# First MLP pair: weight decodes let go one block earlier, token sums spaced evenly from the first one on

## The chip, the cores and the metric

One Trainium2 chip, of which the kernel uses 1 core. The metric is device time in microseconds (us), the median of several executions. Engines are named as the profile names them: PE is TensorE (matmuls), PEld its weight loads, DVE is VectorE, ACT is ScalarE, POOL is GpSimd, SP is SyncE, which here only issues DMAs.

## The reference, cut to what matters

```python
x = attention(q, k, v, omega)            # linear attention, 2304 tokens x 512
xn = x / rms(x) * rms_g
x = (silu(xn @ w_gate) * (xn @ w_val)) @ w_out      # gated MLP, d_ff 1536
h = x @ w_in                                        # second MLP, d_ff 2048
return (h * sigmoid(h)) @ w_out
```

The weights come as 64-bit floats. The kernel reads them as pairs of 32-bit words and turns each 128 x 512 block into a float32 on the chip; this is the "decode" below.

## The kernel before, in words

The 2304 tokens are 18 tiles of 128, in five blocks: j = 0 to 3 with 512 tokens and j = 4 with 256. After attention the normalised tokens lie in `xs[j]` as a high and a low half, so that every product is three matmuls (high x high, high x low, low x high). The rest of the program is a list of groups: nine gated groups of one d_ff block each, then eight groups of the second MLP of two d_ff blocks each. The first two of the eight (`std`, `std + 1`, here called the first and the second MLP pair) are computed plainly. The others, and the gated ones before them, use `quad`: the products of blocks 0 and 1 (and of 2 and 3) are formed from sums and differences of tokens and of weights, with fewer matmuls. The sums of the finished tokens must therefore be made during the two plain pairs, by `token_sums`.

Three streams of side work are interleaved with the matmuls while the program is written out; each engine then runs its own instructions strictly in that written order.

- **Decodes.** `WeightQueue` holds a list of jobs. For one weight block, `dec` issues five DVE operations of 128 x 512 on `raw` and `m` (lines 146, 149, 152, 154, 157) and two POOL additions (L160); then `load` issues the DMA of a later block into the freed `raw` buffer on SP (L134 or L136). `hi` is a copy on ACT (L443) into a weight slot `w0_n` or `w1_n`, `lo` a subtraction on DVE (L447). Matmuls on that weight wait for `lo`. `wq.hold = True` stops jobs from being taken; `need` takes them regardless.
- **Token sums.** `token_sums` gives a list of steps on 128 x 1024: `whole` (DVE, L373), `minus` (DVE, L376), `tok_high` (ACT, L365) and `tok_low` (DVE, L368). They work in temporary slots: ('t', 0), ('t', 1) from the free weight slots, and `w1_7`.
- **The hidden layer.** For each product of 512 tokens, ACT takes the silu (L239 or L713) and a rounded copy (L198) and DVE the remainder (L199); the output matmuls (PE, L300) need both halves. Their results are copied by ACT (L317) to a staging buffer `ya`, which SP stores to HBM (L323) in the first pair and POOL adds to HBM afterwards (L325).

In the first pair the order on PE is: four plain blocks (`mlp_block`, j = 0 and 1), `g1_mlp` of block 2 for both d_ff blocks with the output of blocks 0 and 1 behind them, blocks 3 and 4, then the next pair. The main loop of the program walks `stream()`, whose values `c` are the estimated PE time of the next piece, and decides after each piece whether a sum and a job are taken:

```python
            due += c
            gone += c
            if sums and gone > wq.rest:
                sums.pop(0)()
                gone = gone - wq.rest if wq.rest not in (T_PACE, M_PACE + T_PACE) else 0.0
            if wq.hold:
                due = min(due, M_PACE)
            elif due > wq.pace and wq.tick():
                due = min(due - wq.pace, wq.pace)
```

Of the kernel before, what the change touches and what calls it, by code (L numbers as in the profile page):

```python
# [8 lines left out]
F32 = mybir.dt.float32  # L9
# [11 lines left out]
def kernel(  # L21
# [77 lines left out]
    def ps_tile(which, shape):  # L99
        p, tag, n = pools[which]  # L100
        return p.tile(shape, F32, tag=tag, name=tag, bufs=n)
# [91 lines left out]
    M_PACE, A_PACE, S_PACE, R_PACE, S_REST, T_PACE = 2.0, 1.8, 2.3, 2.0, 2.1, 1.2  # L193
# [39 lines left out]
    def g1_mlp(f, j, hs, mid, late):  # L233
        wq.need((2, "i", f))
        p = ps_tile("ps_g" if blocks[j] == TB * P else "ps_y", [P, blocks[j]])
        yield from proj(wt[2, "i", f], j, p)
        yield from late
        s = pools["s"][0].tile([P, blocks[j]], F32, tag="s", name="s", bufs=pools["s"][1])
        nc.scalar.activation(out=s, in_=p, func=AF.Silu)  # L239
        hs[f] = split_h(s, j)  # L240
        yield from mid
# [87 lines left out]
    tok, sums, ready, wait, stages = {}, [], set(), [], []  # L329
# [6 lines left out]
    std = next(u for u, g in enumerate(groups) if g[0] == 2)  # L336

    def w_tile(side, slot, dtype=F32R):
        pool = pools["w"][2] if side and slot < W_EARLY else pools["w"][side]
        return pool.tile([P, 2 * KC * P], dtype, tag=f"w{side}_{slot}", name=f"w{side}_{slot}")  # L340
# [233 lines left out]
    wq = WeightQueue()  # L574
# [151 lines left out]
    def stream():  # L726
        f0, (f2,) = sweeps[0][1], sweeps[1][1]
        pend = ()
        order = [(3, f0), (4, f0), (1, [f2]), (0, [f2]), (2, [f2]), (3, [f2]), (4, [f2])]
        def temp(k):  # L730
            if k == 2:
                return w_tile(1, 7, F32)
            return rawp.tile([P, KH * TB * P], F32, tag=f"raw{1 - k % 2}", name=f"raw{1 - k % 2}", bufs=1)

        def end(n):
            wq.load(0, n, n)
            wq.hold = n == 0
            wq.rest = T_PACE if wq.hold else M_PACE + T_PACE

        now, later = token_sums(0, temp, end, nc.gpsimd)  # L740
        sums.extend(now)
        for n, (j, fs) in enumerate(order):
            hs, mine = {}, n == len(order) - 1
            for f in fs:
                yield from g1_glu(f, j, hs, () if mine else pend)
                pend = pend if mine else ()
            if n == 2:
                sums.extend(later)
                wq.free += [(0, k) for k in range(6)]
            out = g2_glu(fs, j, hs, j >= NE and fs is f0, False)  # L750
            pend = chain_of(pend, out) if mine else out
        spent = [(1, k) for k in range(3)]
        for u, (kind, fs) in enumerate(groups):
            first, last = kind == 2 and fs[0] == 0, u == len(groups) - 1
            done = u + 1 == std
            wq.rest = S_REST
            wq.std = u < std + NSTD
            wq.pace = A_PACE if u < std else S_PACE if u < std + NSTD else R_PACE
            hs = {j: {} for j in range(NB)}
            if std <= u < std + NSTD:  # L760
                out_of = lambda j: g2_mlp(fs, j, hs[j], first, False, False)
                ys = iter(pend)
                wq.hold = first
                if first:
                    stages[:] = [ya[3][:, n * 1024:][:, :1024] for n in range(2)] + [ya[4]]
                while wait:
                    wait.pop(0)()
                each = [(2, 1), (2, 2), (1, 0), (2, 1)] if first else [(2, 2), (1, 1), (0, 0), (0, 0)]
                for n, k in enumerate(each):
                    if n == 2 and not first:  # L770
                        sums.extend(later + rest)
                    if n == 3:
                        if not first:
                            ys = chain_of(ys, out_of(1))
                        wq.release(*wq.keys(u - 1)[1])
                    j = n // 2 if first else 1 - n // 2
                    yield from mlp_block(fs[n % 2], j, hs[j], ys, k if n < 3 else (k[0], 9))
                yield from g1_mlp(fs[0], 2, hs[2], (), out_of(0) if first else ())
                wq.hold = False
                if first:  # L780
                    assert wq.jobs.pop(0)[0] == 1 << 10
                    now, later = token_sums(
                        0, lambda k: w_tile(1, 7, F32) if k == 2 else wq.slot(("t", k), F32), lambda n: None
                    )
                    sums.extend(now)
                    now, last1 = token_sums(
                        1,
                        lambda k: w_tile(*wq.held["t", 1 - k // 3], F32) if k in (0, 3)
                        else ya[2][:, :2 * KH * TB * P].rearrange("p (k n) -> p k n", k=2)[:, 2 - k],
                        lambda n: None if n else wq.release(("t", 0)),  # L790
                    )
                    sums.extend(now[:9])
                    rest = now[9:]
                yield from g1_mlp(fs[1], 2, hs[2], (), out_of(int(first)))
                yield from g1_mlp(fs[0], 3, hs[3], (), ())
                yield from g1_mlp(fs[1], 3, hs[3], (), out_of(2))
                if not first:
                    sums.extend(last1)
                for f in fs:
                    yield from g1_mlp(f, 4, hs[4], (), ())  # L800
                wq.release(*wq.keys(u)[0])
                pend = chain_of(out_of(3), out_of(4))
                continue
            yield from quad(u, iter(pend), hs)
            if u:
                wq.release(*wq.keys(u - 1)[1])
            else:
                wq.free += spent
            if kind == 1:
                f = fs[0]  # L810
                out_of = lambda j: g2_glu(fs, j, hs[j], False, done)
                ys = chain_of(out_of(0), out_of(1))
                yield from glu_block(f, 2, hs[2], ys, {"g": 0, "v": 1})
                yield from glu_block(f, 3, hs[3], ys, {"g": 1, "v": 1})
                yield from glu_block(f, 4, hs[4], ys, {"g": 1, "v": 1})
                yield from ys
                pend = chain_of(out_of(2), out_of(3), out_of(4))
                wq.release(*wq.keys(u)[0])
            else:
                out_of = lambda j, end=None: g2_mlp(fs, j, hs[j], False, last, end)  # L820
                if u == std + NSTD:
                    wq.release(("t", 1))
                yield from quad(u, chain_of(out_of(1), out_of(0)), hs, 1)
                if last:
                    *stages[:], o0, o1, o2 = [w_tile(1, k, F32) for k in range(3, 9)]
                    ends = [o.rearrange("p (t d) -> p t d", t=2) for o in (o0, o1, o2)]
                    for o, j, n in zip(ends, (4, 2, 2), (0, 0, 1)):
                        for p0, p1, rows in out_pair(j, n):
                            nc.sync.dma_start(out=o[p0:p1], in_=rows)
                    yield from g1_mlp(fs[0], 4, hs[4], (), out_of(3))  # L830
                    yield from g1_mlp(fs[1], 4, hs[4], (), ())
                    yield from chain_of(out_of(4, ends[:1]), out_of(2, ends[1:]))
                else:
                    yield from g1_mlp(fs[0], 4, hs[4], (), out_of(3))
                    yield from g1_mlp(fs[1], 4, hs[4], (), ())
                    wq.release(*wq.keys(u)[0])
                    pend = chain_of(out_of(2), out_of(4))
# [697 lines left out]
    with tc.manual_schedule():  # L1535
# [33 lines left out]
        first = idle(5, [])  # L1569
# [16 lines left out]
        n = 0  # L1586
        for j in range(NE):
            n = add_block(j, sweeps[0][1], n)
# [14 lines left out]
        due = gone = 0.0  # L1603
        for c in stream():
            due += c
            gone += c
            if sums and gone > wq.rest:
                sums.pop(0)()
                gone = gone - wq.rest if wq.rest not in (T_PACE, M_PACE + T_PACE) else 0.0
# [4 lines that stand above are left out]
# [30 lines left out]
```

## Time and profile before

| what | value |
|---|---|
| runs | 952.29 us median of 3 (950.94 to 954.12) |
| the profiled execution | 952.68 us, of which the span from first to last instruction is 950.9 us |
| PE busy | 936.9 us, 99% of the span |
| DVE busy | 699.7 us, 74% |
| ACT, POOL busy | 482.6 us (51%), 452.4 us (48%) |
| chain that ended last | PE 94%, DVE 3%, ACT 1%, issue 1% |
| mean granted clock of PE | 0.996 of full speed |

The page shows one execution. A busy PE there is a PE with matmuls in flight; where it is not busy, the views of waits and of windows tell what it stood waiting for.

### The profile page before, as it was taken

How to read it: one execution, taken by the hardware profiler on the slowest of the kernel's cores; microseconds unless marked ns; L12 is line 12 of the kernel's file. 1: busy time of each engine (PE TensorE's matmuls, PEld its weight loads, DVE VectorE, ACT ScalarE, POOL GpSimd, SP SyncE). 2: the span in 40 equal slices, each digit the busy share in tenths (PEclk: the TensorE clock that was granted, in tenths of full speed). 3: DMA queues.
4: the chain of work that ended last, by engine and by line, in shares of the span. 5: the costliest groups of instructions: out<-in, count | busy, mean ns of one | idle time of the engine just before them, and what ended most of it. 6: DMA issues, size and time to landing. Idle time of an engine off the chain costs nothing.

```text
span 950.9 us, 17234 instructions
## 1 busy us (share of the span) xinstructions
PE 936.9 (99%) x6534; PEld 785.9 (83%) x6534; DVE 699.7 (74%) x1330; ACT 482.6 (51%) x1066; POOL 452.4 (48%) x464
## 2 busy tenths in 40 slices
PE   8999999999999999999999999799999999999998
PEld 6888878888888888888888888688888888888887
DVE  6998989658687878779778787985575757575634
ACT  6999877543424323433333355466444544545442
POOL 8888655315445445426335202536454545454411
PEclk9999999999999999999999999899999999999999
DMA  8655443002111121021112102348768786878777
GB/s 197 166 135 142 137 125 101 12 23 78 56 45 45 45 67 45 23 66 49 41 45 65 47 1 77 123 118 170 142 127 170 128 168 130 162 142 153 116 146 168
DMA packets 89282, 95.03 MB, mean 100 GB/s; under 512 B 28400, under 2 KB 74736, under 8 KB 89200
## 3 DMA queue, kind: packets, MB, share of 16 engines
q1 hardware_dynamic: 79424, 62.41, 22.9%
q0 software_dynamic: 9504, 31.46, 19.8%
q8 instruction: 51, 0.84, 0.4%
q14 instruction: 31, 0.25, 0.1%
q10 hardware_dynamic: 272, 0.07, 0.0%
HBM read 51.45 MB, written 37.75 MB: 94 GB/s over the span
## 4 chain that ended last, share of the span: by engine, by line
PE 94%; DVE 3%; ACT 1%; issue 1%; DMA 0%; SPq 0%; DVEq 0%; ACTq 0%
PE g L580 21%; PE y L300 20%; PE g L205 18%; PE y L259 14%; PE y L205 6%; PE b L1112 4%; PE b L205 4%; PE kv L1192 2%; PE b L1512 2%; PE b L1296 2%; PE b L1085 2%; PE b L1392 1%; PE b L1272 1%; DVE w L373 0%; PE b L1553 0%
## 5 line engine op out<-in xcount | busy, mean ns | idle before, releaser
L160 POOL TENSOR_TENSOR m<-m,raw 128x512 int32<-128x512 int32 x136 | 195.2, 1435 | 210.0 <-issue 83.3
L300 PE MATMUL y<-w,h 128*128 128x512 f32 (+1 forms) x870 | 213.7, 390 | 2.1 <-DVE h L199 1.9
L300 PEld LDWEIGHTS y<-w,h 128*128 128x128 f32 x870 | 163.2, 189 | 36.7 <-DVE h L199 2.5
L205 PE MATMUL g<-xs,w 128*128 128x512 f32 x768 | 188.1, 391 | 4.1 <-DVE w L447 4.1
L205 PEld LDWEIGHTS g<-xs,w 128*128 128x128 f32 x768 | 143.8, 189 | 33.8 <-DVE w L447 4.5
L259 PE MATMUL y<-h,w 128*128 128x512 f32 (+1 forms) x648 | 155.5, 366 | 0.0
L199 DVE TENSOR_TENSOR h<-s,h 128x512 fp32r<-128x512 f32 (+1 forms) x134 | 104.9, 794 | 67.8 <-ACT h L198 66.6
L270 DVE TENSOR_TENSOR ya<-y,ya 128x512 f32<-128x512 f32 (+1 forms) x200 | 122.8, 631 | 20.9 <-PE y L259 20.5
L259 PEld LDWEIGHTS y<-h,w 128*128 128x128 f32 x648 | 113.2, 188 | 20.4 <-DVE h L199 0.5
L580 PE MATMUL g<-xs,w 128*128 128x512 f32 x504 | 128.2, 390 | 0.0
L198 ACT ACTIVATE h<-s 128x512 fp32r<-128x512 f32 (+1 forms) x134 | 77.1, 585 | 89.8 <-DVE s L692 49.4
L325 POOL DMA_DIRECT2D out_dram<-ya x64 | 59.3, 989 | 126.4 <-DVE ya L319 51.1
L580 PEld LDWEIGHTS g<-xs,w 128*128 128x128 f32 x504 | 94.1, 188 | 19.5
L317 ACT ACTIVATE ya<-y 128x512 f32<-128x512 f32 x82 | 48.8, 596 | 77.2 <-PE y L300 77.1
L319 DVE COPY ya<-y 128x512 f32<-128x512 f32 x52 | 35.8, 689 | 62.9 <-PE y L300 62.9
L1161 ACT ACTIVATE e<-b,nb 128x128 f32<-128x128 f32 x272 | 76.1, 425 | 7.6 <-issue 4.1
L447 DVE TENSOR_TENSOR w<-m,w 128x512 fp32r<-128x512 f32 x65 | 64.3, 991 | 13.3 <-ACT w L443 12.1
L580 PE MATMUL g<-w,w 128*128 128x512 f32 x270 | 68.8, 390 | 0.0
L605 ACT ACTIVATE s<-s 128x512 f32<-128x512 f32 x33 | 20.9, 632 | 88.9 <-DVE s L610 88.9
L205 PEld LDWEIGHTS y<-xs,w 128*128 128x128 f32 x480 | 61.5, 188 | 2.7
L205 PE MATMUL y<-xs,w 128*128 128x256 f32 x480 | 62.2, 280 | 0.0
L580 PEld LDWEIGHTS g<-w,w 128*128 128x128 f32 x270 | 50.1, 188 | 10.0
(136 smaller groups left out, 1340.1 us busy)
## 6 DMA issues: line engine op xcount, KB each, us to landing
out_dram<-ya POOLq DMA_DIRECT2D x52, 512.0 KB, 6.9
raw<-in_moe_w_out_dram SPq DMA_DIRECT2D x28, 512.0 KB, 4.1
raw<-in_moe_w_in_dram SPq DMA_DIRECT2D x16, 512.0 KB, 4.4
raw<-in_moe_w_gate_dram SPq DMA_DIRECT2D x12, 512.0 KB, 3.5
raw<-in_moe_w_val_dram SPq DMA_DIRECT2D x12, 512.0 KB, 3.6
qT<-e SPq DMA_DIRECT2D x72, 64.0 KB, 2.4
x<-in_k_dram SPq DMA_DIRECT2D x16, 256.0 KB, 3.8
x<-in_q_dram SPq DMA_DIRECT2D x16, 256.0 KB, 3.3
```

Of the source, the lines that this page charges most:

```text
L160: tt(out=mi, in0=mi, in1=(low if step == 5 else high).bitcast(I32), op=ALU.add)
L198: nc.scalar.activation(out=ht[:, 0, :], in_=s, func=AF.Copy)
L199: nc.vector.tensor_tensor(out=ht[:, 1, :], in0=s, in1=ht[:, 0, :].bitcast(F32), op=ALU.subtract)
L205: nc.tensor.matmul(out=ps, lhsT=w[:, a, cc * P:(cc + 1) * P], rhs=xs[j][:, c, cc, :], start=(n == 0), stop=(n == 3 * KC - 1),)
L259: nc.tensor.matmul(out=ps, lhsT=wt[1, "o", f][:, a, d * P:(d + 1) * P], rhs=hs[f][:, c, :], start=(n == 0), stop=(n == nn - 1),)
L270: nc.vector.tensor_tensor(out=y[:, d, :], in0=ps, in1=y[:, d, :], op=ALU.add)
L300: nc.tensor.matmul(out=ps, lhsT=hs[f][:, a, t * P:(t + 1) * P], rhs=wt[2, "p", f][:, c, d0:d1], start=(n == 0), stop=(n == nn - 1),)
L317: nc.scalar.activation(out=o[:, t % 2, :], in_=ps, func=AF.Copy)
L325: nc.gpsimd.dma_start(out=rows, in_=o[p0:p1], accum_op=ALU.add)
L447: eng.tensor_tensor(out=v[:, 1, :], in0=x, in1=v[:, 0, :].bitcast(F32), op=ALU.subtract)
L580: nc.tensor.matmul(out=ps, lhsT=w[:, a, (c0 + c) * P:(c0 + c + 1) * P], rhs=x(b, c), start=(start and n == 0), stop=(n == 3 * KH - 1), ski ...
L1161: nc.scalar.activation(out=st.e[r][:, :, h, :] if blocks4 else st.e[r][:, h, :], in_=src.rearrange("p (a f) -> p a f", a=4) if blocks4 els ...
```

## The change

`wq.hold` is set to False, and the two slots ('t', 0) and ('t', 1) are taken, before the first `g1_mlp` of block 2 instead of behind it. The counter `gone` no longer runs while there is nothing to sum, so that when a list of sums comes, the first waits for a full interval and each next one too; before, `gone` had grown large and one sum was taken after every piece. In the first pair the interval is 2.4 instead of 2.1.

```diff
-            wq.rest = S_REST
+            wq.rest = 2.4 if u == std else S_REST
...
-                yield from g1_mlp(fs[0], 2, hs[2], (), out_of(0) if first else ())
                 wq.hold = False
                 if first:
                     assert wq.jobs.pop(0)[0] == 1 << 10
+                    for k in range(2):
+                        wq.slot(('t', k), F32)
+                yield from g1_mlp(fs[0], 2, hs[2], (), out_of(0) if first else ())
+                if first:
                     now, later = token_sums(
-                        0, lambda k: w_tile(1, 7, F32) if k == 2 else wq.slot(("t", k), F32), lambda n: None
+                        0, lambda k: w_tile(1, 7, F32) if k == 2 else w_tile(*wq.held["t", k], F32), lambda n: None
                     )
...
-            gone += c
+            gone = gone + c if sums or wq.rest in (T_PACE, M_PACE + T_PACE) else 0.0
```

The programs have the same instructions; PE's rows stand in the same order, with the slots `w0_4` and `w1_0` exchanged. DVE's order differs from the end of the four plain blocks on. Here is DVE before, from the last remainder (L199) of the plain blocks: the remainder of block 2, then sums and the first two decodes.

```order
L199 TENSOR_TENSOR h_7206<-s_7204,h_7206 128x512
L199 TENSOR_TENSOR h_7258<-s_7256,h_7258 128x512
L373 TENSOR_TENSOR w1_0_7262<-xs1_91 128x1024
L146 TENSOR_SCALAR m1_7264<-raw1_6791 128x512
L149 TENSOR_SCALAR raw1_6791<-raw1_6791 128x512
L152 TENSOR_SCALAR m1_7264<-m1_7264 128x512
L154 TENSOR_SCALAR raw1_6791<-raw1_6791 128x512
L157 TENSOR_SCALAR m1_7264<-m1_7264 128x512
L373 TENSOR_TENSOR w0_4_7294<-xs0_90 128x1024
L376 TENSOR_TENSOR w0_4_7294<-w1_0_7262,w0_4_7294 128x1024
```

And DVE at the same place in the changed kernel:

```order
L199 TENSOR_TENSOR h_7206<-s_7204,h_7206 128x512
L146 TENSOR_SCALAR m1_7212<-raw1_6791 128x512
L149 TENSOR_SCALAR raw1_6791<-raw1_6791 128x512
L152 TENSOR_SCALAR m1_7212<-m1_7212 128x512
L154 TENSOR_SCALAR raw1_6791<-raw1_6791 128x512
L157 TENSOR_SCALAR m1_7212<-m1_7212 128x512
L146 TENSOR_SCALAR m0_7251<-raw0_6900 128x512
L149 TENSOR_SCALAR raw0_6900<-raw0_6900 128x512
L152 TENSOR_SCALAR m0_7251<-m0_7251 128x512
L154 TENSOR_SCALAR raw0_6900<-raw0_6900 128x512
L157 TENSOR_SCALAR m0_7251<-m0_7251 128x512
L199 TENSOR_TENSOR h_7280<-s_7278,h_7280 128x512
```

Both decodes now stand ahead of the remainder of block 2 (h_7258 before, h_7280 now) and of the first sum. The second place is DVE up to the low half of `w0_5` (L447), the weight that the second pair's first matmuls read. Before, from the first stored sum (L368) on:

```order
L368 TENSOR_TENSOR w1_6_7364<-w1_0_7262,w1_5_7363 128x1024
L146 TENSOR_SCALAR m1_7391<-raw1_7272 128x512
L149 TENSOR_SCALAR raw1_7272<-raw1_7272 128x512
L152 TENSOR_SCALAR m1_7391<-m1_7391 128x512
L154 TENSOR_SCALAR raw1_7272<-raw1_7272 128x512
L157 TENSOR_SCALAR m1_7391<-m1_7391 128x512
L368 TENSOR_TENSOR w1_4_7389<-w1_7_7324,w1_3_7388 128x1024
L373 TENSOR_TENSOR w1_0_7262<-xs0_90 128x1024
L376 TENSOR_TENSOR w1_0_7262<-w1_0_7262,w1_7_7324 128x1024
L199 TENSOR_TENSOR h_7434<-s_7432,h_7434 128x512
L447 TENSOR_TENSOR w0_5_7420<-m0_7306,w0_5_7420 128x512
```

And in the changed kernel, from the low half of the weight before it; h_7350 is the remainder of block 2 for the second d_ff block, h_7372 that of block 3 for the first:

```order
L447 TENSOR_TENSOR w0_0_7286<-m1_7212,w0_0_7286 128x512
L146 TENSOR_SCALAR m1_7328<-raw1_7220 128x512
L149 TENSOR_SCALAR raw1_7220<-raw1_7220 128x512
L152 TENSOR_SCALAR m1_7328<-m1_7328 128x512
L154 TENSOR_SCALAR raw1_7220<-raw1_7220 128x512
L157 TENSOR_SCALAR m1_7328<-m1_7328 128x512
L376 TENSOR_TENSOR w1_0_7317<-w0_4_7284,w1_0_7317 128x1024
L199 TENSOR_TENSOR h_7350<-s_7348,h_7350 128x512
L373 TENSOR_TENSOR w1_7_7354<-xs1_91 128x1024
L199 TENSOR_TENSOR h_7372<-s_7370,h_7372 128x512
L376 TENSOR_TENSOR w0_4_7284<-w1_7_7354,w0_4_7284 128x1024
L447 TENSOR_TENSOR w0_5_7356<-m0_7251,w0_5_7356 128x512
```

From the first remainder shown above to this L447 the old order has ten operations on 128 x 1024 (four L373, four L376, two L368), the new one five (three L373, two L376); the decodes between are three in both. The third place is ACT where the first `quad` begins; its rows from the second pair's last output tiles to the first copy of `quad` (L592), which a later product of `quad` adds to. Before:

```order
L443 ACTIVATE w0_4_7843<-m1_7667 128x512
L317 ACTIVATE ya4_3690<-y_7845 128x512
L239 ACTIVATE s_7865<-g_7792 128x512
L198 ACTIVATE h_7867<-s_7865 128x512
L365 ACTIVATE xs3_93<-w1_0_7513 128x1024
L239 ACTIVATE s_7884<-y_7870 128x256
L198 ACTIVATE h_7886<-s_7884 128x256
L239 ACTIVATE s_7903<-y_7889 128x256
L198 ACTIVATE h_7905<-s_7903 128x256
L592 ACTIVATE g_7910<-g_7908 128x512
```

In the changed kernel:

```order
L365 ACTIVATE ya2_7842<-w1_0_7802 128x1024
L317 ACTIVATE ya4_3690<-y_7844 128x512
L239 ACTIVATE s_7853<-g_7801 128x512
L198 ACTIVATE h_7855<-s_7853 128x512
L443 ACTIVATE w1_0_7860<-m1_7594 128x512
L239 ACTIVATE s_7874<-y_7858 128x256
L198 ACTIVATE h_7876<-s_7874 128x256
L239 ACTIVATE s_7903<-y_7879 128x256
L198 ACTIVATE h_7905<-s_7903 128x256
L365 ACTIVATE xs3_93<-w0_4_7612 128x1024
L592 ACTIVATE g_7910<-g_7908 128x512
```

Here the copy L443 stands behind the last output tiles instead of ahead of them, since its slot `w1_0` holds a token sum until then, and one more stored sum (L365 of `ya2`) stands in the row.

## Rows read from the trace of the kernel before

**Rows 1.** The page: span, and PE's granted clock in 40 slices.

```profile
span 950.9 us, 17234 instructions
...
PEclk9999999999999999999999999899999999999999
```

**Rows 2.** Who PE waited for, whole span: us in total, times, longest.

```profile
PE g L205 <- DVE w L447: 4.1, 1, 4.1
PE y L300 <- DVE h L199: 1.9, 1, 1.9
```

**Rows 3.** Windows: stretch, its length, busy us of PE, PEld, DVE, ACT, POOL, PE's clock, DMA.

```profile
574.00:582.00 8.00, 8.00 (x37) 6.64 (x36) 2.88 (x7) 5.63 (x12) 0.00 (x0) 1.00 0.19 77
...
594.00:600.00 6.00, 4.09 (x19) 3.06 (x17) 6.00 (x6) 3.18 (x4) 2.24 (x2) 1.00 0.59 163
...
606.00:612.00 6.00, 3.12 (x7) 2.51 (x8) 6.00 (x11) 1.75 (x3) 1.67 (x1) 0.59 0.46 152
```

**Rows 4.** PE's timeline: start, us, line, operation, count, idle before it and its releaser.

```profile
588.28 5.60 PE L205 MATMUL g<-xs,w 128*128 128x512 f32 x24
593.72 1.29 PE L300 MATMUL y<-w,h 128*128 128x512 f32 x5
596.92 4.60 PE L300 MATMUL y<-w,h 128*128 128x512 f32 x19 [1.91 <-DVE h L199]
601.36 2.99 PE L205 MATMUL y<-xs,w 128*128 128x256 f32 x24
604.19 0.63 PE L205 MATMUL g<-xs,w 128*128 128x512 f32 x2
608.88 2.08 PE L205 MATMUL g<-xs,w 128*128 128x512 f32 x4 [4.06 <-DVE w L447]
...
624.52 5.60 PE L205 MATMUL g<-xs,w 128*128 128x512 f32 x24
```

**Rows 5.** DVE's timeline; its operations overlap by about 0.08 us as shown.

```profile
577.10 0.69 DVE L199 TENSOR_TENSOR h<-s,h 128x512 fp32r<-128x512 f32 x1 [0.72 <-ACT h L198]
582.10 0.69 DVE L199 TENSOR_TENSOR h<-s,h 128x512 fp32r<-128x512 f32 x1 [4.31 <-ACT h L198]
582.71 1.22 DVE L373 TENSOR_TENSOR w<-xs 128x1024 f32<-128x1024 f32 x1
...
586.78 2.22 DVE L376 TENSOR_TENSOR w<-w,w 128x1024 f32<-128x1024 f32 x1
588.92 1.53 DVE L146 TENSOR_SCALAR m<-raw 128x512 uint32<-128x512 uint32 x1
590.37 0.42 DVE L149 TENSOR_SCALAR raw<-raw 128x512 uint32<-128x512 uint32 x1
...
657.15 0.69 DVE L447 TENSOR_TENSOR w<-m,w 128x512 fp32r<-128x512 f32 x1 [2.92 <-ACT w L443]
```

**Rows 6.** POOL's timeline: the first pair's first additions, and two with DVE idle.

```profile
585.74 4.42 POOL L160 TENSOR_TENSOR m<-m,raw 128x512 int32<-128x512 int32 x2 [42.65 <-ACT ya L317]
...
654.37 2.71 POOL L160 TENSOR_TENSOR m<-m,raw 128x512 int32<-128x512 int32 x2 [2.36 <-issue]
```

**Rows 7.** ACT's timeline: single operations.

```profile
580.81 0.59 ACT L239 ACTIVATE s<-g 128x512 f32<-128x512 f32 x1
581.44 0.63 ACT L198 ACTIVATE h<-s 128x512 fp32r<-128x512 f32 x1
...
659.02 1.04 ACT L365 ACTIVATE xs<-w 128x1024 fp32r<-128x1024 f32 x1
659.98 0.36 ACT L239 ACTIVATE s<-y 128x256 f32<-128x256 f32 x1
...
661.59 0.58 ACT L592 ACTIVATE g<-g 128x512 f32<-128x512 f32 x1
```

**Rows 8.** DMA issues: kind, count, KB each, median us to landing.

```profile
raw<-in_moe_w_out_dram SPq DMA_DIRECT2D x28, 512.0 KB, 4.1
...
out_dram<-ya SPq DMA_DIRECT2D x8, 512.0 KB, 5.2
```

## Prediction

> **What bounds the kernel now.** The page first: PE's granted clock is full in 39 of 40 slices of a span of 950.9 us; the one lower digit stands at about 600 us [rows 1]. So PE, busy 99% of the time, sets the time, and what can be won without taking matmuls away is what PE loses near that slice. The view of waits names it: in the whole span PE waited once for a low weight half (DVE, L447, 4.1 us) and once for a remainder of the hidden layer (DVE, L199, 1.9 us) [rows 2]. The other waits are at the start of the program and outside the change. PE's timeline puts both in the first MLP pair and between its last matmuls and the second pair's first [rows 4].
>
> How much do they cost? From 588.28 to 624.52 are 36.24 us. In them lie the 24 matmuls of the first row, then 84 of 512 columns and 24 of 256 in twelve rows. At the first row's pace (24 in 593.72 - 588.28 = 5.44, 0.2267 each) the 108 take 24.48; the 24 narrow ones take 604.19 - 601.36 = 2.83. Together 27.31, so **8.93 us are lost**: 1.91 + 4.06 = 5.97 of idle, and 2.96 because the granted clock fell to a mean of 0.59 in the stretch with the longer gap, that is for most of it to 1.2 instead of 2.4 GHz; at the gap of 1.91 it stayed at 1.00 [rows 3, 4].
>
> Why DVE was late: from 574 to 582 it was busy for 2.88 of 8 us, with an idle time of 4.31 before 582.10; from 594 on it is busy for 6.00 of 6 [rows 3, 5]. It starts its burst late and then carries decodes and sums at once.
>
> **The change part by part.** PE's rows keep their order, so its times without a wait can be written down from 588.28. The output block begins at 593.72 and its sixth matmul is the first to read the remainder h_7350: due 593.72 + 5 x 0.2267 = **594.85**. The block ends at 599.16, the narrow products at 601.99; the third matmul after that reads the low half of w0_5: due **602.44**. Then six matmuls, and six more of which the last reads the remainder h_7442: due **604.48**. What stood at 624.52 would stand at 615.59.
>
> *Decodes moved forward.* DVE is free at 577.10 + 0.61 = 577.71. Its prices, from one start to the next: a decode step 0.34 (five are 1.68), an operation of 128x512 0.61 (582.10 to 582.71), one of 128x1024 1.14 (1.22 shown less the 0.08 of overlap) [rows 5]. A POOL addition beside them costs DVE time: an L376 took 2.22 where an L373 of its size took 1.22, a decode step 1.53 instead of 0.42, both while POOL was in its additions [rows 5, 6]; so 1.00 to 1.11 for each addition. Whether an addition lands ahead of a given operation or behind it I cannot see beforehand, so I count one more or less.
>
> Up to the end of h_7350 the new order has three decodes (5.04), two L199 and one L447 (1.83), two L373 and one L376 (3.42): 10.29. Four additions belong to the first two decodes, and one or two of the third fall in: 5.0 to 6.66. End: 577.71 + 15.3 to 16.95 = 593.0 to 594.7, and 0.08 more to be visible, against 594.85. **Cover 0.1 to 1.8 us**; I take the middle, 593.8. The remainder h_7280, ahead of it, is ready from ACT at 582.07 [rows 7], earlier than DVE reaches it after both decodes.
>
> Up to the L447 of w0_5 come one L373, one L376, one L199 and the L447, 3.5: 577.71 + 13.79 + six additions (6.0 to 6.66) = 597.5 to 598.2 against 602.44. Cover over 4 us; this is the wait that cost 4.06 before, when ten instead of five of the large operations stood ahead of it (5 x 1.14 = 5.7) and the work began 4.4 us later.
>
> Up to h_7442 a decode, an L376 and an L199, 3.43, and one or two more additions: 601.9 to 603.8 against 604.48. Cover 0.7 to 2.6.
>
> *Moved on SP.* Each decode ends in a load that waits for POOL's second addition, and SP's queue is in order. The first load now stands ahead of the first store, which goes out at about 582.8 instead of 578.2 and lands 5.2 later, at 588.0 [rows 8]. The copy L317 that reuses that buffer could start at 585.8, so ACT falls 2.2 behind, and is through with the copy, one more L317, a silu (0.59) and the L198 (0.63) of h_7350 by about 590.3 [rows 7]; DVE gets to h_7350 only after 592. Cost nothing; without that cover each us would count. Loads of the later blocks go out some us earlier and take 4.1 [rows 8]: the third decode is reached at 589 and its load leaves at about 582.5, landing 586.6.
>
> *Sums spread.* They are the same operations, later. They have to be done for the first quad, where the new place of L443 on ACT is the risk. By PE's times that quad begins at 651.06 and its fourth product, which needs the copy L592, at 656.50 (six blocks of 24 matmuls behind 615.59 and the narrow products, 2.83, then one more block of 24). On ACT: last output tile 648.23, about 0.2 to start, L317 0.5, L239 0.6, L198 0.63: 650.2. Then DVE's L199 and L368 (1.75): 651.9, L443 0.55, four narrow operations 1.61, L365 1.0, L592 0.58 [rows 7]: **655.7, cover 0.8**. It shrinks by at most 0.6 if DVE's last L376 comes at 648.0: from h_7541, ready at 612.1, DVE has ten of 0.61, fifteen steps and twelve large ones, 24.9, six additions and four of half the size, some 8.9, and about 2 of waits for ACT.
>
> *Interval 2.4 for 2.1 and the earlier slots* add no instruction: nothing by themselves.
>
> The sum: 952.68 for the profiled execution less 8.93 is 943.75; it stands 0.39 above the median, so 943.36 on the runs' scale, and I add 0.2 for covers of a few tenths that may not hold: **943.6 us**.
>
> **A rule against it.** The rows give 1.00 to 1.11 as DVE's delay by one addition. While DVE stood idle before 657.15, two additions took 2.71, 1.36 each [rows 5, 6]. If DVE stood still for the whole of that, h_7350 would end at 577.71 + 10.29 + 6 x 1.36 = 596.2, 1.4 late. The Trainium skill, SBUF — State Buffer, section "Who interferes with whom", says just this: whichever of the two engines issues first gets the shared ports for its whole instruction and the other fully blocks. By that, the sum would be 945.0; by the rows, 943.6. The trace agrees that one blocks, not on the length.
>
> **The rivals.**
> 1. *Short waits stay*: an addition holds DVE for 1.36, or ACT's row at the quad is late by a us. Then h_7350 costs 1.3 to 1.4 of idle, the quad's copy up to another 2; the clock stayed full at a gap of 1.91, so nothing is added for it. 944.5 to 947. For it: covers of 0.1 and 0.3 at the low end. Against: it needs several upper ends together.
> 2. *The backlog only moves* (the change does not do what it says): DVE and POOL have the same work as before, and the stall comes back at h_7442. A gap of 4 us there would bring back the slow clock, 4 + 3 = 7 of the 8.93: 950.4. For it: the work is unchanged. Against: eight additions would have to cost 577.71 + 17.22 + 8b = 608.5, b = 1.7 each, above every row.
> 3. *Slower*: the sums, now later, hold the slot w1_0 until ACT's L443, so the quad's copy is late. It decides from the point where DVE's last L376 ends 9.5 us behind 648.0, at 657.5: then the idle alone eats 8.93, and the low clock adds about 3, 955. For it: all of ACT's copies stand behind that one row. Against: DVE's 36 us of work and delay there fit into the 36 between 612.1 and 648, and most of the additions' delays are upper ends.
>
> **How the numbers follow.** No wait over 0.5 us: 0.62, at 943.6, with a run's own spread 942.3 to 944.6. Rival 1: 0.23. Rival 2: 0.09. Rival 3: 0.06. The lower end is 942.0, since nothing but the 8.93 can be won and the shown runs go down 1.35 from their median; the upper end 948.0 takes in rival 1 and leaves 0.15 above. About 0.3%, 2.9 us, is what a measurement of this kernel can tell from no change: faster 0.85, same 0.09, slower 0.06.
>
> **What would show it.** Right: no row of PE waiting for L447 or L199 in the first pair, the clock at 1.00 in every window from 574 to 660, DVE's first decode at 577.7 instead of after 582, the second quad's rows all some 8.9 us earlier. Wrong: an idle time of PE at the sixth matmul after 593.7 (the additions cost more than I count), at 604, or at the fourth product of the first quad with ACT's copy L592 as releaser.

## The result and the profile after

The changed kernel takes 943.76 us (median of 4 runs, 943.30 to 945.57) against 951.62 for the kernel before in the same series (4 runs, 950.70 to 954.12): a ratio of 0.9917 with an interval of 0.9893 to 0.9941. Forecast were 943.6 us, 942.0 to 948.0, faster. The profiled run took 943.42 us, its span is 941.6 us. In the longest of the four runs, 945.57 us, the mean granted clock is 0.998 instead of 1.000; no trace shows where it lost the clock.

Two lines of the page after, as in [rows 1]; the last one is the granted clock in tenths.

```profile
span 941.6 us, 17236 instructions
...
PEclk9999999999999999999999999999999999999999
```

The waits of PE in the whole span (engine, line, what it waited for: total, times, longest):

```profile
PE b L1556 <- DVE mhalf L1544: 1.4, 1, 1.4
PE b L1299 <- ACT ya L1527: 1.2, 1, 1.2
PE b L1115 <- ACT hl L1103: 1.0, 1, 1.0
...
PE y L300 <- ACT h L198: 0.2, 1, 0.2
```

The two rows of [rows 2] that cost 4.1 and 1.9 us are gone; what is left of a us or more lies at the start of the program. PE's timeline from the last matmuls of the first pair on (start, us, line, operation, count):

```profile
587.98 5.60 PE L205 MATMUL g<-xs,w 128*128 128x512 f32 x24
593.42 5.60 PE L300 MATMUL y<-w,h 128*128 128x512 f32 x24
598.86 2.99 PE L205 MATMUL y<-xs,w 128*128 128x256 f32 x24
601.69 1.55 PE L205 MATMUL g<-xs,w 128*128 128x512 f32 x6
603.09 2.89 PE L300 MATMUL y<-w,h 128*128 128x512 f32 x12
...
615.33 5.60 PE L205 MATMUL g<-xs,w 128*128 128x512 f32 x24
```

No row has a bracket, so no wait is shown there. The stretch that was 36.24 us before [rows 4] is 615.33 - 587.98 = 27.35; forecast were 27.31. The gain of the span is 950.9 - 941.6 = 9.3: 36.24 - 27.35 = 8.89 of it here, and 0.30 because the program's first part ran that much quicker in this execution (587.98 against 588.28).

The windows that answer to [rows 3] (busy time of PE, PEld, DVE, ACT and POOL, then the granted clock, the DMA share and GB/s):

```profile
574.00:582.00 8.00, 8.00 (x37) 6.64 (x36) 6.17 (x18) 5.41 (x11) 2.69 (x1) 1.00 0.00 0
...
594.00:600.00 6.00, 6.00 (x33) 5.14 (x32) 5.97 (x10) 3.49 (x6) 0.64 (x2) 1.00 0.55 175
600.00:606.00 6.00, 6.00 (x35) 5.26 (x34) 5.54 (x6) 4.30 (x9) 3.78 (x2) 1.00 0.14 24
606.00:612.00 6.00, 6.00 (x28) 4.95 (x28) 4.44 (x6) 3.59 (x7) 0.00 (x0) 1.00 0.92 356
```

The clock is 1.00 where it was 0.59, and DVE is busy for 6.17 of the 8 us up to 582, where it was 2.88: the work that came too late was moved there. DVE's timeline shows it:

```profile
577.42 0.42 DVE L146 TENSOR_SCALAR m<-raw 128x512 uint32<-128x512 uint32 x1
...
581.81 0.77 DVE L199 TENSOR_TENSOR h<-s,h 128x512 fp32r<-128x512 f32 x1 [0.95 <-ACT h L198]
582.50 4.58 DVE L373 TENSOR_TENSOR w<-xs 128x1024 f32<-128x1024 f32 x2
587.00 1.79 DVE L447 TENSOR_TENSOR w<-m,w 128x512 fp32r<-128x512 f32 x1
...
591.68 1.77 DVE L199 TENSOR_TENSOR h<-s,h 128x512 fp32r<-128x512 f32 x1
...
597.36 0.68 DVE L447 TENSOR_TENSOR w<-m,w 128x512 fp32r<-128x512 f32 x1
...
601.44 1.25 DVE L199 TENSOR_TENSOR h<-s,h 128x512 fp32r<-128x512 f32 x1 [0.46 <-ACT h L198]
```

The row of 591.68 is h_7350; it ends at 593.45 and is due at 593.42 + 5 x 0.2267 = 594.55, so 1.10 is to spare. The low half of w0_5 (597.36) ends at 598.04, some 4.1 ahead of its matmul, and h_7442 (601.44) at 602.69, 1.5 ahead.

POOL's additions, a row of several instructions running from the first one's start to the last one's end:

```profile
579.32 8.93 POOL L160 TENSOR_TENSOR m<-m,raw 128x512 int32<-128x512 int32 x4 [36.53 <-ACT ya L317]
...
621.38 8.22 POOL L160 TENSOR_TENSOR m<-m,raw 128x512 int32<-128x512 int32 x2 [3.45 <-DVE m L157]
```

Two additions take 8.22 here, and 2.71 where DVE was idle [rows 6]. The experiments come back to this. ACT, at the first store and at the first quad:

```profile
589.40 1.09 ACT L317 ACTIVATE ya<-y 128x512 f32<-128x512 f32 x2 [3.34 <-DMA out_dram<-ya]
...
591.01 0.64 ACT L198 ACTIVATE h<-s 128x512 fp32r<-128x512 f32 x1
...
654.88 0.58 ACT L592 ACTIVATE g<-g 128x512 f32<-128x512 f32 x1
```

The copy L592 ends at 655.46, the matmul that reads it comes at 656.28.

### The profile page after: what moved, and what is told of

Same layout as the page of the kernel before. It is cut to its first block, busy times and chain, and to the rows that moved or that the text cites. A ratio compares the mean times of both kernels' runs of the same rounds, so it can differ in the third digit from the quotient of the medians.

```text
span 941.6 us, 17236 instructions
## 1 busy us (share of the span) xinstructions
PE 933.3 (99%) x6534; PEld 783.7 (83%) x6534; DVE 697.3 (74%) x1330; ACT 481.2 (51%) x1066; POOL 459.5 (49%) x464
## 4 chain that ended last, share of the span: by engine, by line
PE 94%; DVE 1%; POOL 1%; DMA 1%; ACT 1%; issue 0%; SPq 0%; DVEq 0%; POOLq 0%
PE g L580 21%; PE y L300 21%; PE g L205 19%; PE y L259 14%; PE y L205 6%; PE b L1115 3%; PE b L205 2%; PE b L1299 2%; PE kv L1195 2%; PE b L1515 2%; PE b L1088 2%; PE b L1275 1%; PE b L1395 1%; POOL m L160 1%; DVE small L1132 1%; DMA x<-in_q_dram 0%
## 5 line engine op out<-in xcount | busy, mean ns | idle before, releaser
L160 POOL TENSOR_TENSOR m<-m,raw 128x512 int32<-128x512 int32 x136 | 200.3, 1474 | 203.4 <-issue 77.7
L205 PE MATMUL g<-xs,w 128*128 128x512 f32 x768 | 187.0, 389 | 0.0
L205 PEld LDWEIGHTS g<-xs,w 128*128 128x128 f32 x768 | 143.3, 188 | 29.3
L199 DVE TENSOR_TENSOR h<-s,h 128x512 fp32r<-128x512 f32 (+1 forms) x134 | 102.7, 777 | 72.0 <-ACT h L198 71.0
L198 ACT ACTIVATE h<-s 128x512 fp32r<-128x512 f32 (+1 forms) x134 | 77.1, 585 | 89.8 <-DVE s L692 49.4
L447 DVE TENSOR_TENSOR w<-m,w 128x512 fp32r<-128x512 f32 x65 | 65.4, 1007 | 8.6 <-ACT w L443 7.5
L205 PEld LDWEIGHTS y<-xs,w 128*128 128x128 f32 x480 | 61.5, 188 | 2.8
L205 PE MATMUL y<-xs,w 128*128 128x256 f32 x480 | 62.2, 280 | 0.0
```

Of the source, the lines that this page charges most:

```text
L160: tt(out=mi, in0=mi, in1=(low if step == 5 else high).bitcast(I32), op=ALU.add)
L198: nc.scalar.activation(out=ht[:, 0, :], in_=s, func=AF.Copy)
L199: nc.vector.tensor_tensor(out=ht[:, 1, :], in0=s, in1=ht[:, 0, :].bitcast(F32), op=ALU.subtract)
L205: nc.tensor.matmul(out=ps, lhsT=w[:, a, cc * P:(cc + 1) * P], rhs=xs[j][:, c, cc, :], start=(n == 0), stop=(n == 3 * KC - 1),)
L447: eng.tensor_tensor(out=v[:, 1, :], in0=x, in1=v[:, 0, :].bitcast(F32), op=ALU.subtract)
```

## The experiments

Eleven kernels ran in three series, each with the kernel before on the same chip. Line numbers are up to 3 higher in some of them.

**Either half alone.** e1 has the earlier decodes with the old spacing, e2 the new spacing with the old place of the decodes.

```diff
e1, against the changed kernel
-            wq.rest = 2.4 if u == std else S_REST
+            wq.rest = S_REST
-            gone = gone + c if sums or wq.rest in (T_PACE, M_PACE + T_PACE) else 0.0
+            gone += c
e2, against the kernel before
-            wq.rest = S_REST
+            wq.rest = 2.4 if u == std else S_REST
-            gone += c
+            gone = gone + c if sums or wq.rest in (T_PACE, M_PACE + T_PACE) else 0.0
```

> Only the earlier decodes and slots; the sums are still taken one after every piece. My theory, both edits are needed: ahead of the remainder due at the sixth matmul of the output block stand five large operations instead of three, 2.28 us and perhaps one addition (1.1) more than the 1.1 us of cover that the changed kernel's trace shows there, so 1.2 to 2.3 us of idle; ahead of the next one ten instead of six, another 1 to 2.5. Idle 2.5 to 4.5 in all, 946 to 948 us, with or without a fall of the clock. Rival, the decodes' start alone does it: no wait for L199 or L447, 943.5 us.

> Only the even spacing of the sums; decodes and slots start where they did. My theory: DVE again idles until 582.1; up to the remainder due at 594.85 stand 8.0 us of work and three or four additions, 593.4 to 594.6, no wait or one of a few tenths; up to the low half of w0_5 8.7 us and two or three additions more, 604.3 to 606.5 against 602.44, so PE waits 2 to 4 us for L447 and the clock may fall: 945.5 to 949 us. Rival, the spacing alone does it: no wait, 943.5 us.

e1: 950.22 us, ratio 0.9988 (0.9976 to 0.9999). e2: 949.70 us, 0.9976 (0.9964 to 0.9988). So by the medians the halves give 1.3 and 1.8 us of the 7.9 that they give together. PE, POOL and ACT of e1:

```profile
607.64 0.73 PE L300 MATMUL y<-w,h 128*128 128x512 f32 x2 [3.09 <-ACT h L198]
609.00 2.63 PE L300 MATMUL y<-w,h 128*128 128x512 f32 x7 [0.63 <-DVE h L199]
...
593.36 15.03 POOL L160 TENSOR_TENSOR m<-m,raw 128x512 int32<-128x512 int32 x4 [4.64 <-ACT h L198]
...
605.81 0.63 ACT L443 ACTIVATE w<-m 128x512 fp32r<-128x512 f32 x1 [5.53 <-POOL m L160]
```

In e1 the stall moved from L447 to the next hidden remainder, h_7442, the place that the prediction's second rival names, but through another engine than I had expected: POOL's four additions took 15 us, ACT stood 5.5 us at the copy L443 that needs them, and the L198 behind it in ACT's row came late. The idle time, 3.72, lies in the expected 2.5 to 4.5. The time lies above the expected 946 to 948, which was to hold with a fall of the clock too: the clock fell to 0.82 and 0.89 in the two windows of 6 us from 606 on, some 1.7 us more (6 x 0.18 + 6 x 0.11), and the range had too little room for it. PE of e2:

```profile
607.26 1.20 PE L205 MATMUL g<-xs,w 128*128 128x512 f32 x4 [3.02 <-DVE w L447]
```

There the old wait for L447 is 3.02 instead of 4.06, within the expected 2 to 4, and the clock still falls (0.73 from 606 to 612). The time is 0.7 above the expected range.

**The interval.** e3 is the changed kernel with the interval 2.1 (S_REST).

> Both edits, with the interval of 2.1 instead of 2.4. One large operation more (seven instead of six) stands ahead of the remainder due at 604.2, which the changed kernel's DVE finished about 1.6 us early; the other two due rows have the same rows ahead of them. My theory: 0 to 0.8 us of idle, 943.4 to 944.3 us. Rival, the 2.4 carries the gain: a wait of 2 us or more there, 946 us.

Measured: 946.39 us, 0.9940 (0.9923 to 0.9957), 2 us more than expected. That is the rival's time, but not at the rival's place: the first pair has no wait; a new one stands in the second pair. POOL, DVE (a window, then the row at which the addition gets in), ACT and PE of e3:

```profile
619.06 8.46 POOL L160 TENSOR_TENSOR m<-m,raw 128x512 int32<-128x512 int32 x1 [12.64 <-DVE m L157]
...
618.00:624.00 6.00, 6.00 (x29) 4.95 (x28) 6.00 (x12) 1.87 (x3) 4.94 (x1) 1.00 0.36 89
...
626.38 2.21 DVE L376 TENSOR_TENSOR ya<-ya 128x1024 f32<-128x1024 f32 x1
...
629.79 0.63 ACT L443 ACTIVATE w<-m 128x512 fp32r<-128x512 f32 x1 [8.90 <-POOL m L160]
...
635.03 0.73 PE L300 MATMUL y<-w,h 128*128 128x512 f32 x2 [1.17 <-ACT h L198]
636.06 4.61 PE L300 MATMUL y<-w,h 128*128 128x512 f32 x19 [0.30 <-DVE h L199]
```

One addition is 8.46 us under way, while DVE's operations follow one another without a gap from 615.42 to 626.35; ACT's copy waits 8.90, and L198 behind it makes PE wait. The expectation had no term for a sum that goes in a piece earlier in the second pair.

**The cover of h_7350.** e4 is the changed kernel; it issues the second sum of the list (L373) four times instead of once.

```diff
-            nc.vector.tensor_tensor(out=u[k], in0=half(j, 0, h), in1=half(j, 1, h), op=ALU.add)
+            for _ in range(4 if (p, k, eng) == (0, 0, nc.vector) else 1):
+                nc.vector.tensor_tensor(out=u[k], in0=half(j, 0, h), in1=half(j, 1, h), op=ALU.add)
```

> The changed kernel with the second sum (the 128x1024 addition of block 0's halves) made four times over, to the same value: three operations of 1.14 us put ahead of the remainder due at the sixth matmul, which had 1.1 us of cover. My theory, DVE's row sets that wait: PE idles 3.4 - 1.1 = 2.3 us there, up to 3.4 if an addition of POOL moves in front as well; 945.8 to 947 us if the clock stays full, about 2 us more if it falls. Rival, that remainder waits for ACT and the store's landing and DVE has room: no idle, 943.5 us.

Measured: 947.11 us, 0.9946 (0.9931 to 0.9961). PE of e4, and the window around its wait:

```profile
596.97 5.99 PE L300 MATMUL y<-w,h 128*128 128x512 f32 x19 [2.40 <-DVE h L199]
...
594.00:600.00 6.00, 3.60 (x10) 2.60 (x9) 6.00 (x6) 1.65 (x3) 3.76 (x2) 0.72 0.13 25
```

Three times 1.14 less the cover of 1.10 is 2.32; the wait is 2.40, at the matmul that was expected. The clock fell to 0.72 in the window around it, and the time lies just above the 945.8 to 947 given for a full clock.

**Does a gap on DVE let POOL in?** e5 and e9 are e3 with a chain of four tiny dependent DVE operations behind the decodes; in e5 it stood, by a mistake of mine, only behind the eight decodes ahead of the stretch at issue, in e9 behind the two in it. The edit of e9:

```diff
                 for k in range(7):
                     w_decode((0, 0, key, None), st[key], k, n)
+                    if k == 4 and u == std + NSTD and key in (a0, a1):
+                        for _ in range(4):
+                            nc.vector.tensor_scalar(out=g_sb[:, :1], in0=g_sb[:, :1], scalar1=1.0, scalar2=None, op0=ALU.mult)
```

> The kernel of e3 (changed kernel with the interval 2.1), with four tiny DVE operations on 128 x 1, each of which reads the result of the one before it, behind the last decode step (L157) of every decode of both pairs. They leave short idle times on DVE and take some tenths of a us each decode; nothing of the result changes. Theory A (POOL's additions come in only where DVE stands idle for a moment; in e3 they stood from 619.06 to 627.52 behind DVE operations that followed one another without a gap, ACT's L443 waited for them, and the L198 of the hidden layer behind it made PE wait 1.17 + 0.30): the first addition of that decode ends within 2 us of its L157 instead of 8.46, ACT's L443 no longer waits 8.9, the two waits of PE (1.47) are gone, 0.5 at most remains; time 943.6 to 945.2. Theory B (DVE has too much work in that stretch, whatever the order in which POOL and DVE get in): the additions cost DVE the same 1.0 to 1.1 each, earlier, PE waits 1 to 2.5 us for DVE's L199 in place of ACT's L198; time 946 to 948.

> The kernel of e3 (interval 2.1) once more with the four tiny dependent DVE operations, now behind the last step of the two decodes (those of the first quad's d_ff blocks) whose additions were kept out in e3; in e5 they stood behind the eight decodes ahead of these, and the stretch at issue was untouched. In e5 a tiny chain let an addition in within 0.2 us, and two took 2.75 to 3.54. Theory A: the two additions behind the decode at about 618.5 end within 4 us instead of 10.7, ACT's L443 waits under 2 us instead of 8.9, and the 1.17 + 0.30 that PE waited at about 635 are gone (0.3 at most stays); time 943.6 to 945.3, about 1.5 below e3. Theory B (DVE's load there is the cause): PE waits 1 to 2 us for DVE's L199 at the same matmuls; time as e3, 946 to 947.5.

e5: 946.09 us, 0.9944 (0.9925 to 0.9962). e9: 946.66 us, 0.9954 (0.9938 to 0.9971). DVE and POOL of e5, at the first decode and in the untouched stretch, and its new wait:

```profile
579.45 0.71 DVE L442 TENSOR_SCALAR g_sb<-g_sb 128x1 f32<-128x1 f32 x4
580.08 1.18 DVE L146 TENSOR_SCALAR m<-raw 128x512 uint32<-128x512 uint32 x1
581.18 1.53 DVE L149 TENSOR_SCALAR raw<-raw 128x512 uint32<-128x512 uint32 x1
...
579.67 2.75 POOL L160 TENSOR_TENSOR m<-m,raw 128x512 int32<-128x512 int32 x2 [36.52 <-ACT ya L317]
618.54 13.68 POOL L160 TENSOR_TENSOR m<-m,raw 128x512 int32<-128x512 int32 x4 [12.98 <-DVE m L157]
...
606.16 1.89 PE L300 MATMUL y<-w,h 128*128 128x512 f32 x7 [1.42 <-DVE h L199]
```

The chain of 0.71 us lets the additions in at once: two take 2.75, about 1.37 each, and the two decode steps that follow are longer by 0.76 and 1.11. Without a chain, in the same run, four additions still take 13.68. In e9 the chain works there as well (rows of POOL, ACT and PE):

```profile
616.93 3.55 POOL L160 TENSOR_TENSOR m<-m,raw 128x512 int32<-128x512 int32 x2 [12.26 <-ACT h L198]
...
620.51 0.63 ACT L446 ACTIVATE w<-m 128x512 fp32r<-128x512 f32 x1 [1.38 <-POOL m L160]
...
622.22 4.61 PE L300 MATMUL y<-w,h 128*128 128x512 f32 x19 [0.53 <-DVE h L199]
...
631.41 1.06 ACT L365 ACTIVATE ya<-ya 128x1024 fp32r<-128x1024 f32 x1 [3.95 <-DVE ya L376]
...
634.18 5.33 PE L300 MATMUL y<-w,h 128*128 128x512 f32 x21 [1.24 <-ACT h L198]
```

So one half of my theory stands (a gap lets POOL in), and the other fell: the time did not change. ACT waits 3.95 us for a sum (L376) where it waited 8.90 for POOL, and PE loses 0.53 + 1.24 instead of 1.17 + 0.30. Theory B, that DVE and POOL have too much work together there, fits this, but neither run shows it, because the chains are work for DVE as well: each holds it for 0.63 us (579.45 to 580.08 above). Two of them, 1.3 us, stand ahead of the late sum of e9, and four, 2.5 us, ahead of h_7442 in e5, which PE waited 1.42 for. What the additions let in early would have cost without the chains stays open.

**Without the additions.** In e6 (e1) and e7 (the kernel before) they have 4 columns instead of 512.

```diff
+            b = (low if step == 5 else high).bitcast(I32)
+            if part:
+                mi, b = mi[:, :4], low.bitcast(I32)[:, :4]
-            tt(out=mi, in0=mi, in1=(low if step == 5 else high).bitcast(I32), op=ALU.add)
+            tt(out=mi, in0=mi, in1=b, op=ALU.add)
```

> The kernel of e1 (only the hold and the slots moved), with the POOL additions of the decodes of both pairs cut from 512 to 4 columns and the shift by 3 ahead of them left out, so that the weights of the second MLP are other finite numbers (the result is not the reference's). Theory A (what made PE wait 3.7 in e1 is the additions: three delays of 1.0 to 1.1 for DVE up to the last, and nine us in which a pending addition kept ACT's L443 and the L198 behind it): no wait of PE over 0.3 in the first pair, the clock at 1.00, time 943.3 to 944.8. Theory B (the sums in a row are late by themselves): PE still waits 1.5 to 3 for DVE's L199 at the same row, 945.5 to 949.

> The kernel before, with the POOL additions of the decodes of both pairs cut from 512 to 4 columns and the shift by 3 ahead of them left out (the weights of the second MLP are other finite numbers, the result is not the reference's). In the trace of before six additions delayed DVE up to the low half of w0_5: three operations took 2.20 to 2.22 for 1.21, a decode step 1.53 for 0.42, two L199 1.77 for 0.68, 6.3 us together; four of them, 4.2, lie ahead of the remainder that PE waited 1.91 for. Theory A (each addition costs DVE 1.0 to 1.1, as the prediction counted): the remainder comes 2.3 early, the low half of w0_5 at about 602.5 against a due time of 602.44, so waits of 0 to 0.8 in all, 943.3 to 945.0. Theory B (the late start of DVE's burst and the ten large operations are the cause, the additions a small part): a wait of 2 to 4 us stays at L447, and with it some slow clock, 946 to 950.

e6: 943.50 us, 0.9922 (0.9901 to 0.9944). e7: 944.11 us, 0.9923 (0.9905 to 0.9940). Neither shows a wait of PE in either pair that a bracket marks, and the clock stays full there. DVE of e7, with the old order (L379 and L450 are the old L376 and L447), and PE (L208 is L205) at the first matmuls of the second pair:

```profile
586.76 1.23 DVE L379 TENSOR_TENSOR w<-w,w 128x1024 f32<-128x1024 f32 x1
...
601.87 0.68 DVE L450 TENSOR_TENSOR w<-m,w 128x512 fp32r<-128x512 f32 x1
...
601.97 1.83 PE L208 MATMUL g<-xs,w 128*128 128x512 f32 x6
```

The first row took 2.22 before [rows 5]. The low half of w0_5 is done at 602.55; expected was 602.5. PE's six matmuls there take 1.83 instead of 1.55 in the changed kernel, so it waited some 0.3. But for that, the whole loss of the kernel before is thus undone by taking the additions' 6.3 us off DVE, with the old order, the late start and the ten large operations left as they were.

**Longer intervals.** e8 has 3.0 and e11 2.5 in place of 2.4; e10 is e8 with one job more taken in the first quad.

```diff
e10, against e8
-        wq.tick()
+        wq.tick() and u == std + NSTD and wq.tick()
```

> The changed kernel with the interval 3.0 instead of 2.4 in the first pair. One sum fewer stands ahead of h_7350 and of the low half of w0_5, and the sums end later. Theory A (2.4 is no narrow optimum; what counts is that nothing is taken in a row ahead of the due rows, and the second pair has room for sums that come later): no wait of PE in the first pair, none over 0.5 in the second, 943.2 to 944.4. Theory B (sums that come later fill DVE without gaps in the second pair, POOL's additions and with them ACT's L443 and L198 are kept, as in e3, or the quad's copy L592, 0.8 early in the changed kernel, comes late): PE waits 0.7 to 2.5 us at the second pair's second output block (about 632) or at the quad, 944.5 to 947.

> The kernel of e8 (interval 3.0) with one job more taken in the first quad behind the two plain pairs, so that the list of jobs is not one behind in the five groups that follow; apart from this group their DVE rows are those of the changed kernel but for the names of two slots. Theory A (e8's loss is the one job by which the list stayed behind: a sum holds the slot ('t', 0) one piece longer, the job that needs a free slot is not taken, and in every later group the last low half, L447, is written out only where it is needed, 3.73 late): the waits of PE for L447 in the five later groups are gone, 0 to 2.5 us stay in the first quad; time 943.2 to 948. Theory B (the late sums delay DVE itself): waits of over 3 us stay in several groups; time over 955.

> The changed kernel with the interval 2.5 instead of 2.4. Written out, the sum that gives the slot ('t', 0) back comes one piece (1.3 us of estimated PE time) later than with 2.4, behind the last point at which the job that waits for a free slot can be taken in the second pair, and the list stays one job behind as with 3.0. Theory A (2.4 lies just ahead of that edge, and the edge is a step): PE waits some 3.7 us for L447 in each of the five later groups, time 965 to 975, as with 3.0. Theory B (what cost time with 3.0 grows with the interval): a few tenths to 5 us over the changed kernel, 943.5 to 949.

e8: 973.21 us, 1.0231 (1.0213 to 1.0249), far outside of both expectations. PE of e8, the first two of five such rows:

```profile
674.25 0.72 PE L300 MATMUL y<-w,h 128*128 128x512 f32 x2 [2.43 <-DVE w L447]
...
724.68 1.22 PE L300 MATMUL y<-w,h 128*128 128x512 f32 x2 [3.73 <-DVE w L447]
```

The pairs lose 0.3 us; PE then waits in five later groups, 18.0 us together with shorter ones, and the clock is 0.50 behind such a wait (724 to 730). The cause is in how the program is written out: `quad` takes a fixed number of jobs, and the job that needs a free slot finds none if the sum that releases ('t', 0) comes one piece later. The list then stays one job behind to the end. e11, with 2.5, is written out the same way: 974.68 us, 1.0249 (1.0232 to 1.0266), and PE waits 19.3 us for L447. e10: 950.92 us, 0.9997 (0.9984 to 1.0011), between the ranges of the two theories; of the waits for L447 one is left, in the first quad:

```profile
676.99 1.22 PE L300 MATMUL y<-w,h 128*128 128x512 f32 x2 [4.12 <-DVE w L447]
```

The other four are gone with one job, as theory A had it; the one left is longer than the 2.5 that I allowed. Its 4.12, a wait of 0.4 in the first pair and the clock of 0.72 from 676 to 682 (6 x 0.28 = 1.7) are 6.2 of the 7.2 us that it lies over the changed kernel.

## Why the prediction was right

- *What is lost before, 8.93:* right for the profiled execution; 8.89 came back in that stretch, idle time and clock together. The runs gained 7.9, the sum has 8.7 (952.29 less 943.6). Its 952.29 is a median of three; the later medians of the kernel before are 951.17 to 951.62. Among its 39 runs beside the experiments, the 8 with a mean clock of 0.996, as in the profiled one, average 952.8 us, the 31 with 0.998 951.2. So that execution lost more to the clock than most.
- *Decodes moved, h_7350:* the end was forecast at 593.8, with the 0.30 by which this execution was early 593.5; it is 593.45, and e4 confirms the cover of 1.1. That it is met so closely is luck, for two errors cancel in it: DVE did reach h_7280 before ACT had it, and stood 0.95 us, which the step denied; and four additions cost DVE time, not five to six, since the first one (POOL's row from 579.32) ran while DVE stood.
- *The price of an addition, 1.00 to 1.11:* right. The rows of after show it (1.79 and 1.77 for 0.68, 2.33 for 1.22), and e7 undid six of them to within 0.1 of the sum. The Trainium skill, SBUF — State Buffer, section "Who interferes with whom", has the loser block for the whole instruction, which I weighed at 1.36 each; measured is 1.0 to 1.1 of DVE per addition. That the wait of 1.4 for h_7350 did not come does not settle it: with four additions in place of six, 1.36 each would have ended h_7350 at 593.45 + 4 x 0.26 = 594.5, just about in time too. The same section says that issue order decides who blocks. The traces agree only in part: in e3 the addition that starts at 619.06 does not get ahead of DVE operations that start after it, up to 626.38; in e5 one that a gap lets in holds the next DVE step up, 0.76 us longer.
- *w0_5 and h_7442:* covers of 4.1 and 1.5, forecast over 4 (4.2 at least by its bounds) and 0.7 to 2.6.
- *SP:* the first store left at 584.16, not 582.8, and ACT was through with h_7350's L198 at 591.65, not by 590.3 (590.0 with the shift of 0.30). DVE came to it at 591.68: of the cover of 1.7 or more named there 0.03 was left, and any more would have come out of the 1.10 of h_7350.
- *Quad:* the copy ends 0.82 ahead of its matmul, forecast 0.8.
- *Interval "nothing by themselves":* wrong as a general statement. 2.1 costs 2.6 us over 2.4 by the medians of different series, and 2.5 costs 31. At 2.4 both are avoided, which the prediction had not worked out: that 2.4 is a good number is luck, as far as the prediction goes. Its third rival, sums that come later and hold a slot, is what happens at 2.5, but by another slot (('t', 0), not w1_0) and through the list of jobs: its "point from which it decides", 9.5 us, is in truth one piece of the written order.

Why the change gains as much as it does: DVE and POOL have 6.3 us of mutual blocking ahead of a due weight; the earlier decodes fill most of an idle time of DVE of 4.31 us [rows 5], and the spacing takes five large operations away from ahead of w0_5. Alone, each leaves a wait over 3 us, and the clock falls with it.

## What to carry to other kernels

Count what two engines that block one another need together up to a due time (e7: 6.3 us less, and the stall is gone). Letting the waiting one in earlier (e5, e9) moved the stall and saved nothing, though there the means cost DVE time as well. Where one half of a change leaves a stall long enough to cost the clock, its gain shows only with the other half, so trying halves one by one misleads. After a change of pacing, look for steps that were skipped for want of a slot: a list that falls one behind costs in every later group, and the edge may be next to the chosen number.

## What was not expected of the hardware

In these traces a waiting POOL addition did not get in between DVE operations that followed each other without a gap: 8.46 us in e3 for one, against 1.37 when a chain of dependent operations left it room. A gap of 0.03 us was enough (626.35 to 626.38 in e3; the row behind it takes 2.21 instead of 1.22). Once one is in, additions and DVE's operations take turns: the next addition lengthens the next DVE operation (0.76 and 1.11 us in e5).

The clock did not follow the length of PE's gap alone. It stayed at 1.00 in the windows around gaps of 1.17 (e3), 1.42 (e5), 1.91 [rows 3] and 2.43 (e8, 672 to 678), and fell around gaps of 2.40 (e4, 0.72), 3.02 (e2, 0.73) and 3.73 (e8, 0.50). The window of 2.43 is this one, to be set beside that of e4 above:

```profile
672.00:678.00 6.00, 3.75 (x17) 3.12 (x18) 5.97 (x11) 1.20 (x2) 4.38 (x4) 1.00 0.65 87
```

What decides between 2.40 and 2.43 was not tried.
